# Chunk-end decays of a gated linear recurrence: one 32-partition transpose and four copies, against four transposes that write to their own partitions

## The chip, the cores and the metric

One core of one Trainium2 chip. The metric is the device time of one execution in microseconds (us), the median over several executions. The engines are TensorE (PE, with its weight loads shown apart as PEld), VectorE (DVE), ScalarE (ACT), GpSimd (POOL) and SyncE (SP); the last two issue most of the DMAs.

## The reference

```
batch, n_heads, seq, head_dim = (4, 8, 768, 48);  n_tokens, d_model, d_ff = (3072, 384, 2048)

state = zeros((B, H, D, D))
for t in range(S):
    state = alpha[:, :, t, :, None] * state + einsum('bhd,bhe->bhde', k[:, :, t], v[:, :, t])
    y[:, :, t] = einsum('bhd,bhde->bhe', q[:, :, t], state)

x = y.transpose(0, 2, 1, 3).reshape(B * S, H * D)
h = x @ w_in
g = 0.5 * h * (1.0 + tanh(sqrt(2 / pi) * (h + 0.044715 * h * h * h)))
return g @ w_out                                    # float32, 3072 x 384
```

A recurrence over 768 steps, in which each of the 48 features of a head decays by its own `alpha`, is followed by a two-layer feed-forward net.

## The kernel before

The sequence is cut into 6 chunks of 128 steps. A chunk of two batches is a unit; the 12 units have numbers m = 0 to 11 (chunk c = m // 2, batch pair i = m % 2), and a task's name holds its unit: `mask6.0` is the first mask of unit 6.

For one unit, ACT takes the logarithm of alpha (`ln`), PE sums it along the chunk (`cum`), ACT makes the running decay b = exp(cum) (`b`) and its inverse (`binv`), and DVE scales q by b (`qp`) and k by binv (`kp`). Both are turned so that features lie on partitions: on PE for units 0 to 4, by two DMA transposes issued from SP for units 5 to 11 (`turn`, line 546). PE makes the scores (`attn`, line 583; it also starts the outputs with the carried state, line 563), DVE masks them in four pieces (`mask`, line 590), PE finishes the outputs (`y`, lines 640 and 648), `x` copies them out of PSUM, and the turned x (`xT`) feeds layer 1 on PE (`l1`, line 683, 8 steps for each unit), ACT's `gelu` (line 689), and layer 2 on PE (`l2`, line 702, 8 steps for each unit), whose sums are copied out (`ot`, line 714) and stored from SP (`store`, line 727). `l16.2` is step 2 of layer 1 of unit 6.

The state is carried from chunk to chunk: PE makes k-transposed times v (`kv`, line 600), and DVE computes (kv + old state) * decay over the whole chunk (`st`, lines 622 and 625). That needs the last row of b with its features on partitions. For units 0 to 2 PE sums them in another way. For units 3 to 9 (`ROW_ENDS`) the task `rows` does it on DVE. b is a tile of 128 tokens by 768 values in float32; its last row is on partition 127. `row_ends` transposes the last 32 partitions in blocks of 32x32 into the tile `turned` (1024 elements on each of partitions 96 to 127), so that the last token becomes the last column of each block. Four copies (lines 467 and 468) then take these columns to partitions 0, 32, 64 and 96 of a small tile `rows`: even heads go to partitions 0 to 47, odd heads to 64 to 111. The task `end` (line 610) spreads the result over the two heads of a pair, and both `st` of the unit read that.

The order of the work on each engine is not written in loops: tasks with dependencies, costs and ranks go through a list scheduler when the kernel is built. The table `W` holds the cost it believes of each kind of task, `SHIFT` moves the rank of single tasks, `AFTER` adds dependencies that only fix an order, and `FIRST` writes out the order of roughly the first 40 us. Each engine then runs its own list in order. A task also waits for a buffer: `BUFS` gives the number for each tag. PSUM has four buffers of the tag `ff` (layer 1, layer 2 and half of the scores), two of `yk` (outputs, `kv`, turned x) and one double one of `ca`.

POOL issues the loads (line 337); before some of them it waits until a turned tile has landed (`gate`, line 351, steps such as 'hold k 8').

Of the kernel before, what the change touches and what calls it, by code (L numbers as in the profile page):

```python
# [7 lines left out]
F32 = mybir.dt.float32  # L8
# [8 lines left out]
    cum=530, cum_packed=1500, t8=450, t4=225, attn=340, kv=170, inter=165, intra=203, tx=168, l1_4=655, l1_2=340, l2=651,  # L17
    qk2=880, qk1=500, ev8=610, ev4=350, mask=610, st=1065, st0=545, end=110, attn2=600, vb=320, vb_act=480, ring=1300, ring_issue=670, out=2050, lead=600, receipt=1400, receipt_hw=1000, xc=475, xe=275, ot=540,
    ev8_act=920, ev4_act=520, xc_act=385, xe_act=400, ot_act=450,
    strip=1700, cast=1450, weight=2080, dma=2100, issue=1100, wissue=760, sp=420, store=2600, turn=1250, landed=2200, xbar_qk=1500, xbar_x=1400, turn_lead=50, stored=300, turn_receipt=200, rows=1600, ones=205, late_qk=1700, late_x=1700, late_x6=500, piece=330, late_k=1500, piece_issue=450, begin=620, cast_0=1300, share=1200, cast_1=1900, ln_packed=1040, cold=380, t64=640, fill=216, zero=1100,  # L20
)
COST = {
    ("ACT", "b"): (385, 135), ("ACT", "binv"): (385, 135), ("ACT", "ev"): (600, 40), ("ACT", "gelu"): (510, 110),
# [151 lines left out]
class _Kernel:  # L175
# [58 lines left out]
    PIECES = (0, 192, 320, 384)  # L234

    SHIFT = {
        'cum5.0': 100, 'ev4.1': 97, 'kp6.0': 1515, 'kp9.0': -3, 'kv3.0': -140, 'kv4.1': -540, 'mask3.0': 183, 'mask3.1': 300, 'mask6.3': 2077,
        'qp5.0': 1077, 'qp7.0': 57, 'qp8.0': 110, 'rows4.0': 450, 'rows7.0': -164, 'rows9.0': -280, 'tx3.1': -340, 'tx4.1': -727, 'x6.0': -7088,
        'x6.1': -7042,
    }  # L240

    AFTER = {
        'attn8.0': 'l17.2', 'kv6.1': 'l25.4',
    }

    ROW_ENDS = (3, 4, 5, 6, 7, 8, 9)

    URGENT = (2,)
    BUFS = dict(rows=3, turned=1, ca=1, yk=2, ff=4, la=3, qp=4, kp=4, b8=2, kn=2, qkT=4, atm=6, x=3, ot=4, bend=3, ends=8,
                a=5, q=5, k=5, vb=5)  # L250

    def __init__(self, ctx, tc, q, k, v, alpha, w_in, w_out, out):
        nc = self.nc = tc.nc
        self.tc, self.out = tc, out
        B, H, S, D = q.shape
        self.B, self.H, self.S, self.D = B, H, S, D
        C = self.C = 128
        self.NCH = S // C
        self.src = {"a": alpha, "q": q, "k": k, "v": v}
        self.w_in_dram, self.w_out_dram = w_in, w_out  # L260
        self.d_model, self.d_ff = w_in.shape
        self.NKT, self.NFT = self.d_model // C, self.d_ff // C

        self.const = ctx.enter_context(tc.tile_pool(name="const", bufs=1))
        self.sb = ctx.enter_context(tc.tile_pool(name="sb", bufs=1))
        self.ps = ctx.enter_context(tc.tile_pool(name="ps", bufs=1, space=bass.MemoryType.PSUM))

        const = self.const
        self.ut_h = const.tile([C, C], F16, name="ut_h")
        self.ut = const.tile([C, C], BF16, name="ut")  # L270
        self.gate = const.tile([C, 1], F32, name="gate")
        self.ut_blk = [const.tile([C, C], F16, name=f"ut_blk{i}") for i in range(2)]
        self.blk = const.tile([C, 4], F16, name="blk")
        self.ident = const.tile([C, C], BF16, name="ident")
        self.ones = const.tile([C, 1], F16, name="ones")
        self.zero = const.tile([C, 512], BF16, name="zero")
        self.half = const.tile([C, 2], F32, name="half")
        self.w_in = [const.tile([C, self.NKT, self.d_ff // 4], BF16, name=f"w_in{i}") for i in range(4)]
        self.w_out = const.tile([C, self.NFT, self.d_model], BF16, name="w_out")
        self.state = [[const.tile([C, H // 2, 2 * D], BF16, name=f"st{b}_{i}") for i in range(2)]  # L280
                      for b in range(B)]
        self.ring = {n: [const.tile([C, 2, H, 64], F16 if n == "la" else BF16, name=f"{n}{i}")
                         for i in range(self.BUFS[n])] for n in ("la", "qp", "kp")}
        self.used = {n: 0 for n in (*self.ring, "rows", "b")}
        self.bs = [const.tile([C, 2 * H * D + 16], F32, name=f"b{i}") for i in range(self.BUFS["b8"])]
        self.rows = [const.tile([C, 32], F32, name=f"rows{i}")[:, 0:H].rearrange("f (i p) -> f i p", i=2) for i in range(self.BUFS["rows"])]
        self.NX = 3
        self.xT = [const.tile([C, B, self.NKT, C], BF16, name=f"xT{c}") for c in range(self.NX)]
        self.NG = 2
        self.gT = [const.tile([C, self.NFT, B * C], BF16, name=f"gT{i}") for i in range(self.NG)]  # L290
        self.eng = {"ACT": nc.scalar, "DVE": nc.vector}

    def tile(self, tag, shape, dt, name=None):
        pool = self.ps if tag in ("ca", "yk", "ff") else self.sb
        return pool.tile(shape, dt, tag=tag, bufs=self.BUFS[tag], name=name or tag)

# [133 lines left out]
    def exp(self, u, n, lo, hi):  # L430
        D, H = self.D, self.H

        def emit(e):
# [7 lines left out]
            else:  # L441
                if n not in u:
# [4 lines left out]
                    else:  # L447
                        u[n] = self.sb.tile([self.C, 2, H, D], BF16, tag=n, bufs=self.BUFS["b8"], name=n)
                cum = u["cum"][lo][:, None, 0:H * D] if u["packed"] else u["cum"][:, lo:hi, 0:H * D]
# [4 lines left out]
    def row_ends(self, u):  # L454

        C, H, D = self.C, self.H, self.D
        nc = self.nc

        def emit(e):
            b, t = u["b_row"], self.tile("turned", [C, 2, H // 2, 2, 2, 32], F32, "b_turned")  # L460
            to = u["bend"] = self.rows[self.used["rows"] % len(self.rows)]
            self.used["rows"] += 1
            last = b[C - 32:C]
            nc.vector.transpose(t[C - 32:C].rearrange("t i p o b c -> t (i p o) b c"),  # L464
                                bass.AP(last.tensor, last.offset, [list(last.ap[0]), [D, 2 * H], [32, 2], [1, 32]]))
            for o in range(2):
                nc.vector.tensor_copy(to[64 * o:64 * o + 32], t[C - 32:C, :, :, o, 0, 31])
                nc.vector.tensor_copy(to[64 * o + 32:64 * o + D], t[C - 32:C - 32 + D - 32, :, :, o, 1, 31])
        return emit

    def scaled(self, u, n, lo, hi):
# [133 lines left out]
    def ends(self, u):  # L605
        C, H = self.C, self.H

        def emit(e):
            t = u["ends"] = self.tile("ends", [C, 2, H // 2, 2], F32)
            self.nc.vector.tensor_tensor(  # L610
                t.rearrange("f i p o -> f (i p) o"), u["bend"].rearrange("f i p -> f (i p)")[:, :, None].to_broadcast([C, H, 2]),
                self.half[:, None, :].to_broadcast([C, H, 2]), op=ALU.mult)
        return emit

# [115 lines left out]
    def tasks(self):  # L730
        s = self.s = Scheduler(self.BUFS, self.fill, 40000, self.FIRST, self.LANDED)
        B, NCH = self.B, self.NCH
# [283 lines left out]
    def run(self):  # L1016
        nc, C = self.nc, self.C
        self.tasks()
        nc.vector.memset(self.zero, 0.0)
        nc.vector.memset(self.ones, 1.0)  # L1020
        make_upper_triangular(nc, self.ut_h, val=1.0, diag=True)
        first = self.p[0, 0]["q"] = self.tile("q", [C, 2, self.H, self.D], F32)
        nc.vector.memset(first[:, 0, 0, 0:1], 0.0)
        make_identity(nc, self.ident)
        nc.vector.memset(self.half, 0.0)
        for o in range(2):
            nc.vector.memset(self.half[64 * o:64 * o + 64, o:o + 1], 1.0)
        nc.vector.tensor_reduce(self.blk, self.ident.rearrange("p (g j) -> p j g", j=4), axis=mybir.AxisListType.X, op=ALU.max)
        same = self.blk[:, None, :].to_broadcast([C, C // 4, 4])
        nc.vector.tensor_tensor(self.ut_blk[1].rearrange("p (g j) -> p g j", j=4), self.ut_h.rearrange("p (g j) -> p g j", j=4), same, op=ALU.mult)  # L1030
        nc.vector.tensor_tensor(self.ut_blk[0], self.ut_blk[1], self.ident, op=ALU.subtract)
        for i in range(max(self.BUFS[n] for n in self.ring)):
            for n in self.ring:
                if i < self.BUFS[n]:
                    nc.vector.memset(self.ring[n][i][:, :, :, self.D:64], 0.0)
        nc.vector.tensor_copy(self.ut, self.ut_h)
        for t in self.rows:
            nc.vector.memset(t, 0.0)
        for t in self.bs:
            nc.vector.memset(t[:, 2 * self.H * self.D:], 0.0)  # L1040
        order = self.s.order()
        for t in order:
            if t.load == LN_EXP:
                self.act_set(LN_EXP)
            t.emit(t.engine)
# [30 lines left out]
```

## Time and profile before

| what | value |
|---|---|
| median of three timed runs | 176.02 us (175.55, 176.02, 178.0) |
| profiled execution | 174.84 us, span 173.1 us, granted PE clock 1.000 |
| PE busy | 166.8 us, 96% of the span |
| ACT busy | 129.0 us, 75% |
| DVE busy | 105.2 us, 61%; nine tenths or more of nearly every slice from 47 to 74 us |
| POOL busy | 60.1 us, 35% |
| `rows`: 7 transposes | 8.7 us, 1241 ns each |
| `rows`: 28 copies | 6.0 us, 164 to 168 ns at the median, 880 ns at most |

The profile is one execution. The span runs from its first to its last instruction; the execution's own time is 1.74 us longer. In the timeline a group of matmuls is given with its modelled end, which reaches some 0.16 us past the start of the next group when PE runs without a gap: in such a row the next start, not the end, tells how fast PE goes. "Idle before" is counted from that modelled end.

### The profile page before, as it was taken

How to read it: one execution, taken by the hardware profiler on the slowest of the kernel's cores; microseconds unless marked ns; L12 is line 12 of the kernel's file. 1: busy time of each engine (PE TensorE's matmuls, PEld its weight loads, DVE VectorE, ACT ScalarE, POOL GpSimd, SP SyncE). 2: the span in 40 equal slices, each digit the busy share in tenths (PEclk: the TensorE clock that was granted, in tenths of full speed). 3: DMA queues.
4: the chain of work that ended last, by engine and by line, in shares of the span. 5: the costliest groups of instructions: out<-in, count | busy, mean ns of one | idle time of the engine just before them, and what ended most of it. 6: DMA issues, size and time to landing. Idle time of an engine off the chain costs nothing.

```text
span 173.1 us, 4474 instructions
## 1 busy us (share of the span) xinstructions
PE 166.8 (96%) x1847; PEld 130.2 (75%) x1847; DVE 105.2 (61%) x220; ACT 129.0 (75%) x212; POOL 60.1 (35%) x71
## 2 busy tenths in 40 slices
PE   7999999999999999999989999999999999999993
PEld 2666999666887795797777787787696796886973
DVE  6399920166889999895995697996950735100000
ACT  4578999756979888869679869868699892581831
POOL 2396446995645500810802503900800300000000
PEclk9999999999999999999999999999999999999999
DMA  4999999999999999799698996999899892401102
GB/s 135 308 252 214 203 241 236 239 228 203 228 301 198 255 238 110 138 204 163 166 246 135 165 218 141 169 252 204 185 174 167 97 177 48 119 18 45 49 0 91
DMA packets 54452, 30.11 MB, mean 174 GB/s; under 512 B 42528, under 2 KB 50848, under 8 KB 54432
## 3 DMA queue, kind: packets, MB, share of 16 engines
q0 software_dynamic: 26464, 17.70, 61.7%
q1 hardware_dynamic: 27424, 11.74, 33.9%
q10 hardware_dynamic: 544, 0.39, 0.9%
q8 instruction: 14, 0.23, 0.6%
q14 instruction: 6, 0.05, 0.1%
HBM read 25.17 MB, written 4.72 MB: 173 GB/s over the span
## 4 chain that ended last, share of the span: by engine, by line
PE 76%; DVE 10%; ACT 6%; DMA 3%; issue 2%; SPq 0%; DVEq 0%
PE hT L683 32%; PE acc L702 28%; PE at L583 3%; DMA a<-in_alpha_dram 2%; DVE b_turned L464 2%; DVE atm L590 2%; PE qkT_ps L488 2%; PE yps L648 2%; DVE stmp L622 1%; DVE st L625 1%; PE kv L600 1%; PE cum L416 1%; PE yps L563 1%; PE idle L318 1%; PE xT_ps L671 1%
## 5 line engine op out<-in xcount | busy, mean ns | idle before, releaser
L683 PE MATMUL hT<-xT,w_in 128*128 128x256 bf16 x576 | 68.2, 273 | 1.1 <-DVE atm L590 0.8
L702 PE MATMUL acc<-w_out,gT 128*128 128x384 bf16 (+3 forms) x416 | 68.8, 314 | 0.0
L689 ACT ACTIVATE gT<-hT 128x512 bf16<-128x512 f32 x96 | 55.4, 602 | 11.7 <-PE hT L683 8.0
L683 PEld LDWEIGHTS <-w_in 128*128 128x128 bf16 x576 | 61.4, 114 | 3.3 <-issue 1.4
L702 PEld LDWEIGHTS <-gT 128*128 128x128 bf16 x416 | 37.2, 98 | 19.6
L590 DVE TENSOR_TENSOR atm<-at,ut 128x512 bf16<-128x512 f32 x48 | 30.3, 683 | 4.8 <-PE at L583 4.6
L714 ACT COPY ot<-acc 128x384 f32<-128x384 f32 (+3 forms) x21 | 9.3, 446 | 17.2 <-PE acc L702 14.6
L351 POOL CAST gate<-qkT 128x1 f32<-128x1 bf16 x6 | 2.1, 353 | 51.4 <-DMA qkT<-kp 51.4
L478 DVE TENSOR_TENSOR kp<-k,binv 128x768 bf16<-128x768 f32 (+1 forms) x15 | 11.9, 793 | 11.0 <-ACT binv L450 10.6
L478 DVE TENSOR_TENSOR qp<-q,b 128x768 bf16<-128x768 f32 (+1 forms) x15 | 11.9, 792 | 8.4 <-ACT b L450 8.4
L337 POOL DMA_DIRECT2D k<-in_k_dram x11 | 12.2, 1108 | 6.0 <-DMA vb<-in_v_dram 3.3
L337 POOL DMA_DIRECT2D q<-in_q_dram x11 | 12.2, 1112 | 4.6 <-DMA k<-in_k_dram 1.2
L337 POOL DMA_DIRECT2D vb<-in_v_dram x11 | 12.3, 1116 | 3.8 <-PE kv L600 1.1
L337 POOL DMA_DIRECT2D a<-in_alpha_dram x11 | 12.3, 1115 | 3.5 <-DMA w_in<-in_moe_w_in_dram 1.3
L450 ACT ACTIVATE b<-cum 128x768 f32<-128x768 f32 (+1 forms) x15 | 10.3, 688 | 2.6 <-PE cum L418 1.5
L309 ACT ACT_TABLE_LOAD x9 | 11.5, 1283 | 0.9 <-PEq L1060 0.7
L689 ACT ACT_TABLE_LOAD x9 | 11.5, 1283 | 0.2
L622 DVE TENSOR_TENSOR stmp<-kv,st 128x384 f32<-128x384 f32 x16 | 8.9, 554 | 3.2 <-PE kv L600 3.0
L450 ACT ACTIVATE binv<-cum 128x768 bf16<-128x768 f32 (+1 forms) x15 | 10.3, 686 | 0.5 <-PE cum L388 0.5
L658 DVE CAST x<-yps 128x384 bf16<-128x384 f32 x9 | 4.9, 556 | 8.2 <-PE yps L648 8.2
L464 DVE STREAM_TRANSPOSE b_turned<-b 32x1024 f32<-32x1024 f32 x7 | 8.7, 1241 | 1.7 <-ACT b L450 1.6
L625 DVE TENSOR_TENSOR st<-stmp,ends 128x384 bf16<-128x384 f32 x16 | 8.9, 558 | 0.6
(86 smaller groups left out, 152.8 us busy)
## 6 DMA issues: line engine op xcount, KB each, us to landing
out_dram<-ot SPq DMA_DIRECT2D x19, 192.0 KB, 3.7
a<-in_alpha_dram POOLq DMA_DIRECT2D x9, 384.0 KB, 8.9
q<-in_q_dram POOLq DMA_DIRECT2D x9, 384.0 KB, 8.6
k<-in_k_dram POOLq DMA_DIRECT2D x9, 384.0 KB, 7.0
vb<-in_v_dram POOLq DMA_DIRECT2D x9, 192.0 KB, 9.6
w_in<-in_moe_w_in_dram POOLq DMA_DIRECT2D x4, 384.0 KB, 9.3
w_out<-in_moe_w_out_dram POOLq DMA_DIRECT2D x4, 384.0 KB, 11.1
out_dram<-ot SPq DMA_DIRECT2D x9, 96.0 KB, 4.6
```

Of the source, the lines that this page charges most:

```text
L309: nc.scalar.add_instruction(mybir.InstLoadActFuncSet(name=nc.get_next_instruction_name(), act_func_set_id=i, engine=mybir.EngineType.Activ ...
L337: dma(u[t][:, lo:hi].rearrange("t b h d -> t (b h) d"), src.rearrange("b h s d -> s (b h) d")[c * C:(c + 1) * C])
L450: self.nc.scalar.activation(u[n].rearrange("t i h d -> t i (h d)")[:, lo:hi], cum, AF.Exp, scale=1.0 if n == "b" else -1.0)
L464: nc.vector.transpose(t[C - 32:C].rearrange("t i p o b c -> t (i p o) b c"), bass.AP(last.tensor, last.offset, [list(last.ap[0]), [D, 2 * ...
L478: self.nc.vector.tensor_tensor(out, rows, b, op=ALU.mult)
L590: self.nc.vector.tensor_tensor(u["atm", i][:, o], u["at", i][o], self.ut[:, None, :].to_broadcast([self.C, self.H // 2, self.C]), op=ALU.mult)
L622: nc.vector.tensor_tensor(s, acc, old, op=ALU.add)
L625: nc.vector.tensor_tensor(new.rearrange("f p (o d) -> f (p o) d", o=2), acc.rearrange("f p (o d) -> f (p o) d", o=2), ends, op=ALU.mult)
L683: self.nc.tensor.matmul(h[:, s], w_in[:, j, nt % 4 + s], self.xT[c % self.NX][:, lo:hi, j], start=j == 0, stop=j == self.NKT - 1, skip_gro ...
L689: return lambda e: self.nc.scalar.activation(self.gT[c % self.NG][:, nt:nt + 2, lo * self.C:hi * self.C], f.pop(("h", c, lo, nt)), AF.Gelu ...
L702: self.nc.tensor.matmul(f["acc", c, b][:, lo:hi], self.gT[c % self.NG][:, nt, b * self.C:(b + 1) * self.C], self.w_out[:, nt, lo:hi], star ...
L714: self.copy(e)(f["ot", c, b][:, sl], f["acc", c, b] if half is None else f["acc", c, b, half][:, sl])
```

## The change

The transpose and the four copies of `row_ends` become four transposes. Each takes the 32 values of one half (features 0 to 31 or 32 to 63; the second half runs into the next head's values, as before) of all 8 even or all 8 odd heads, reads them in steps of two heads, 256 elements on each of 32 partitions, and writes straight to the partitions of `rows` where these features belong. `rows` grows to 128 x 8 x 32; the decays are its last column, [:, :, 31], which `end` now reads in steps of 32 elements. The tile `turned` and the clearing of `rows` at the start go.

The cost of `rows` in the scheduler's table goes from 1600 to 1400, and `SHIFT` and `AFTER` are new, so the order of tasks changes on PE, DVE, ACT and SP from about 52 us on. POOL's order stays, and so does all that `FIRST` writes out.

```diff
-        'cum5.0': 100, 'ev4.1': 97, 'kp6.0': 1515, 'kp9.0': -3, 'kv3.0': -140, 'kv4.1': -540, 'mask3.0': 183, 'mask3.1': 300, 'mask6.3': 2077,
-        'qp5.0': 1077, 'qp7.0': 57, 'qp8.0': 110, 'rows4.0': 450, 'rows7.0': -164, 'rows9.0': -280, 'tx3.1': -340, 'tx4.1': -727, 'x6.0': -7088,
-        'x6.1': -7042,
+        'b10.0': 10, 'binv8.0': -10, 'ev4.1': -154, 'kp6.0': 1801, 'kp7.0': -13, 'kp9.0': -347, 'ln5.0': -1426, 'mask10.0': -50, 'mask3.1': 340,
+        'mask8.0': 200, 'mask8.1': 36, 'qp4.0': -217, 'qp5.0': 10, 'qp8.0': 10, 'st4.0': 870, 't4.0': -633,
...
-        'attn8.0': 'l17.2', 'kv6.1': 'l25.4',
+        'b4.0': 'binv4.0', 'kv8.1': 'l27.2',
...
-        self.rows = [const.tile([C, 32], F32, name=f"rows{i}")[:, 0:H].rearrange("f (i p) -> f i p", i=2) for i in range(self.BUFS["rows"])]
+        self.rows = [const.tile([C, H, 32], F32, name=f"rows{i}") for i in range(self.BUFS["rows"])]
...
-            b, t = u["b_row"], self.tile("turned", [C, 2, H // 2, 2, 2, 32], F32, "b_turned")
-            to = u["bend"] = self.rows[self.used["rows"] % len(self.rows)]
+            t = self.rows[self.used["rows"] % len(self.rows)]
             self.used["rows"] += 1
-            last = b[C - 32:C]
-            nc.vector.transpose(t[C - 32:C].rearrange("t i p o b c -> t (i p o) b c"),
-                                bass.AP(last.tensor, last.offset, [list(last.ap[0]), [D, 2 * H], [32, 2], [1, 32]]))
+            last = u["b_row"][C - 32:C]
             for o in range(2):
-                nc.vector.tensor_copy(to[64 * o:64 * o + 32], t[C - 32:C, :, :, o, 0, 31])
-                nc.vector.tensor_copy(to[64 * o + 32:64 * o + D], t[C - 32:C - 32 + D - 32, :, :, o, 1, 31])
+                for half in range(2):
+                    f = 64 * o + 32 * half
+                    nc.vector.transpose(t[f:f + 32], bass.AP(last.tensor, last.offset + o * D + 32 * half,
+                                                             [list(last.ap[0]), [2 * D, H], [1, 32]]))
+            u["bend"] = t[:, :, 31]
...
+            last = u["bend"] if u["m"] in self.ROW_ENDS else u["bend"].rearrange("f i p -> f (i p)")
             self.nc.vector.tensor_tensor(
-                t.rearrange("f i p o -> f (i p) o"), u["bend"].rearrange("f i p -> f (i p)")[:, :, None].to_broadcast([C, H, 2]),
+                t.rearrange("f i p o -> f (i p) o"), last[:, :, None].to_broadcast([C, H, 2]),
...
-        for t in self.rows:
-            nc.vector.memset(t, 0.0)
```

The pieces of the new order that the prediction uses, each engine's list read from left to right:

```
DVE before: rows3 st2.1 mask3.2 mask3.3 end3 mask3.0 mask3.1 st3.1 xe3.1 qp4 kp4 xe3.0 st3.0 rows5 ev4.0 kp5 ev4.1 end5 rows4 mask4.0-4.3 end4
DVE after:  rows3 st2.1 mask3.0 mask3.2 mask3.3 end3 mask3.1 x3.1 x3.0 kp4 qp4 xe3.1 rows4 ev4.1 ev4.0 end4 kp5 st3.0 st3.1 rows5 mask4.0-4.3
DVE before: st5.0 st5.1 rows7 mask6.0-6.2 kp7 end7 qp7 mask6.3 x6.0 st6.0 rows8 st6.1 ot5.1 kp8 mask7.0-7.3 end8 qp8
DVE after:  st5.0 st5.1 kp7 qp7 mask6.0-6.3 rows7 x6.1 end7 st6.0 st6.1 kp8 rows8 mask7.0-7.3 qp8 x7.0 end8
DVE before: st8.0 st8.1 rows9 ot6.1 kp9 qp9 end9 mask8.0-8.3
DVE after:  st8.0 mask8.2 mask8.3 mask8.1 mask8.0 ot6.1 x8.0 kp9 qp9 rows9 end9
PE before:  l16.0 l16.1 attn7 l16.2-16.4 l16.5 l16.6 y7 l16.7 l26.0 kv7.0 kv7.1 l26.1 l26.2 kv8.0 l26.3 cum9 kv8.1 l26.4-26.7 l17.0-17.3 attn8
PE after:   attn7 l16.0-16.4 y7 l16.5 l16.6 kv7.0 kv7.1 l16.7 l26.0 kv8.0 l26.1-26.3 attn8
SP before:  turn8 (k), turn8 (q), turn7 (x)          SP after: turn8 (k), a store of unit 5, turn8 (q), turn7 (x)
```

## The prediction

> **What bounds the kernel now.** I read the page first, then PE's timeline for places where it waits, then DVE's and POOL's for the reason, then SP's.
>
> ```profile
> span 173.1 us, 4474 instructions
> ...
> PE 166.8 (96%) x1847; PEld 130.2 (75%) x1847; DVE 105.2 (61%) x220; ACT 129.0 (75%) x212; POOL 60.1 (35%) x71
> ...
> L464 DVE STREAM_TRANSPOSE b_turned<-b 32x1024 f32<-32x1024 f32 x7 | 8.7, 1241 | 1.7 <-ACT b L450 1.6
> ```
>
> PE sets the end. A cut in DVE time is worth only what PE loses to DVE. PE's timeline shows where that is:
>
> ```profile
> 67.58 0.86 PE L648 MATMUL yps<-vb,atm 128*128 128x48 bf16 x16
> ...
> 69.61 0.33 PE L671 MATMUL xT_ps<-ident,x 128*128 128x128 bf16 x3 [0.18 <-DVE x L658]
> ...
> 87.79 4.09 PE L683 MATMUL hT<-xT,w_in 128*128 128x256 bf16 x36 [0.79 <-DVE atm L590]
> ...
> 100.18 0.60 PE L583 MATMUL at<-qkT 64*128 64x128 bf16 x15 [0.17 <-DVE ot L714]
> ...
> 113.72 0.81 PE L683 MATMUL hT<-xT,w_in 128*128 128x256 bf16 x6 [0.30 <-DVE ot L714]
> ```
>
> The printed idle time starts at a modelled end, 0.16 us after the point where the next group could have started, so each wait costs 0.16 more: 0.34, 0.95, 0.33 and 0.46. The first row, y4, lasts 0.86 where the later groups of this kind last 0.56: 0.30 of waiting inside it. With 0.20 at 94.89 (where `cum8` waits for ACT) PE loses 0.30 + 0.34 + 0.95 + 0.33 + 0.46 + 0.20 = 2.58 us after 50 us. After 114 us it loses nothing to DVE. That is the ceiling of any gain here, 1.5% of the time.
>
> The two largest losses stand behind `rows`:
>
> ```profile
> 84.32 1.24 DVE L464 STREAM_TRANSPOSE b_turned<-b 32x1024 f32<-32x1024 f32 x1
> 85.60 0.16 DVE L467 COPY rows<-b_turned 32x8 f32<-32x8 f32 x1
> 85.77 0.16 DVE L468 COPY rows<-b_turned 16x8 f32<-16x8 f32 x1
> 85.95 0.88 DVE L467 COPY rows<-b_turned 32x8 f32<-32x8 f32 x1
> 86.84 0.17 DVE L468 COPY rows<-b_turned 16x8 f32<-16x8 f32 x1
> ```
>
> POOL's timeline at the same time:
>
> ```profile
> 85.67 1.16 POOL L337 DMA_DIRECT2D a<-in_alpha_dram  x1
> ```
>
> The third copy ends at 86.83, exactly with this POOL row. A copy at 111.92 (0.80 us) ends likewise at 112.72 with the POOL row of 111.57. The transpose of 110.47 lies wholly under POOL rows and takes its usual 1.24.
>
> **What one `rows` costs.** Before: five of the seven run 2.01 us from first start to the next instruction's start (59.16 to 61.17), the two with a blocked copy 2.72 and 2.64.
>
> After: four transposes of 32x256; no row shows one. DVE's time grows by 1.04 ns for each element (kp: 553 ns for 384 elements, 953 for 768), so the transpose of 1024 is 1065 + 176 fixed, and one of 256 is 266 + 176 = 442 ns. Do neighbours overlap? The copies, with no wait between the last three, start 0.17 to 0.18 apart while each lasts 0.16 to 0.17: no overlap. Memsets at the start do overlap:
>
> ```profile
> 2.62 0.17 DVE L1035 MEMSET la<- 128x128 uint32 x1
> 2.76 0.17 DVE L1035 MEMSET qp<- 128x128 uint32 x1
> ```
>
> The copies write to different groups of 32 partitions in turn; the memsets don't. The four transposes do as the copies, so I take no overlap and a gap of 0.015: 4 x 0.457 = 1.83 us, 0.18 less than 2.01. With the overlap of the masks (0.08 a piece) it would be 4 x 0.36 = 1.45. Outer bounds: 4 x 0.31 = 1.24, if a quarter of the elements takes a quarter of the time, and 4 x 1.24 = 4.96 if size didn't matter, which the kp rows speak against; the latter, behind which three `rows` stand before y4, would lose PE some 15 us.
>
> The Trainium skill (VectorE: DVE Perf Modes, section "Two Vector instructions with no wait between them") says that an instruction whose output starts in another quadrant than the last one's waits until all earlier ones are done. That speaks against the change: the splitting into four pays the fixed part four times. By it the sum is 1.83, without it 1.45.
>
> The same skill (SBUF — State Buffer, section "Who interferes with whom") lists copies among the operations that lock a port shared with GpSimd, one blocking the other; it doesn't list the transpose there. By it the 0.7 us accidents go with the copies; else they may return.
>
> **What goes and what stays, with the new order.** Times are those of the trace, shifted by each edit.
> - `rows7` is no longer ahead of `mask6.0`. Instead kp7 and qp7 are (0.87 each): 84.30 + 1.75 = 86.05, mask done 86.74; layer 1 needs its buffer at 86.84. Loss 0.95 becomes 0.
> - `ot6.1` no longer stands behind `rows9` (it precedes it): 0.46 becomes 0. `ot5.1` goes from behind `rows8` to ACT, and `cum8` comes one step later, when its input is there: 0.33 and 0.20 become 0.
> - y3.1's mask3.3 comes third: 51.93 - 0.18 + 2 x 0.60 + 0.68 + 0.06 (release) = 53.69 against 53.63: 0.06.
> - Ahead of unit 4's masks, DVE gets two casts from ACT (x3, 0.46 each), gives up one `xe` (0.27), and saves 0.18 on each of rows3, 4 and 5: +0.11. y4's loss goes from 0.30 to 0.41; the 0.34 behind it stays. No gain in the stretch where DVE is fullest.
> - `rows7` now stands between mask6.3 (88.46) and x6.1: x6.1 is done 88.46 + 1.83 + 0.55 = 90.84; kv6.1, which needs its buffer, could go at 90.67. New loss, with release, 0.23.
> - `rows8` now stands between kp8 and mask7.0. cum8 is one layer-2 step (0.65) and one kv (0.17) later, and so are ACT's exponentials: kp8 ends 98.2, rows8 100.03, mask7.0 100.71. attn7 has moved ahead of l16.0 and starts at 98.18, so l16.2 wants mask7.0's buffer at 100.24: new loss 0.46.
> - The cleared `rows` tiles (three memsets, 0.1 us) lie in DVE's free time from 4.3 to 6.5; `end` reads as many elements as before.
>
> Sum: 0.06 + 0.41 + 0.34 + 0.23 + 0.46 = 1.50 lost in place of 2.58: 1.1 us gained, 174.84 to 173.7 on the profiled execution (span 172.0, and the 1.74 around it as before). That one is 1.2 us below the median of the timed runs, 176.02, and below all three; I carry the difference over: 174.9.
>
> **Rivals.**
> 1. The transposes overlap (1.45). Three rows of 0.38 less take y4's loss and most of the 0.34 behind it away, kv6.1's too, and l16.2's falls to 0.08: some 0.3 left, 2.3 gained, 173.7 at the median. For it: nothing depends on a neighbour; against: the copies.
> 2. No cheaper: with 2.01 for one `rows` the losses are 0.24 + 0.95 + 0.34 + 0.41 + 0.64 = 2.58: no change, 176.0. For it: each instruction pays the fixed part.
> 3. Slower, by one mechanism: attn8 waits for its turned q. It moves ahead by ten PE steps. Before, SP issued that turn at 104.36, it landed 2.7 us later, and attn8 went at 114.68: 7.6 us to spare. After, from the end of mask7.0, DVE has three masks and qp8 ahead of the turn, 2.8 us; PE has six layer-1 steps, y7, four layer-2 steps and three kv, 3.93 + 0.40 + 2.60 + 0.51 = 7.44. PE waits if landing takes over 4.6 us, and the kernel gets slower than before from 5.7.
>
> ```profile
> 104.36 1.23 SPq L546 DMA_TRANSPOSE qkT<-qp  x1
> ```
>
> The fourteen turns land in 2.7 to 7.7 us, the slow ones with loads on the queues. At 7.7 the price is 3.1 - 1.1 = 2.0: 178.0. A store now goes between the two turns of unit 8, which speaks for it; against it, the loads of that time (k9, issued at 96.6, 6.6 us) have nearly landed, and the next ones are held until unit 8's k has. I expect about 4. The turns of unit 11 meet the same rule: attn11 moves ahead by one step of 0.65, of 1.1 to spare; both late would make 179.5 or more.
>
> **How the numbers follow.** Chances: forecast 0.45, rival 1 0.14, rival 2 0.12, rival 3 0.29. The time is the forecast's, 174.9. The range goes down to rival 1 with 1.2 us for the runs' excess over the profiled one, 172.5, and up over 178.0 towards both turns late, 178.6. The bound of 2%, about what a measurement of this kernel can tell from no change, is 3.5 us. Faster by that needs rival 1 and a steadier course of the runs: 0.15. Slower by it needs rival 3 at both places, or more at one: 0.23. The rest, 0.62, is within.
>
> **What would show it.** A 32x256 transpose of 0.44 us, with starts 0.46 apart (0.36: rival 1); none longer under POOL's rows. The 14.7 us that DVE is busy in `rows` (8.7 + 6.0) become 28 x 0.442 = 12.4. PE's waits at 87 and 113 us are gone, y4's stays, a small one before l16.2 is new. A PE wait at attn8 released by the DMA of qkT is rival 3. The forecast is wrong if PE's new waits sum to over 2.6 us, or if a wait appears that no piece above names.

## The result, and the profile after

The changed kernel takes 174.26 us at the median of 18 runs, the kernel before 175.16 beside it; the ratio is 0.994 (95% interval 0.9915 to 0.9966). That is 1.0 us less (0.6 to 1.5), inside the bound of 2%. Forecast were 1.1 us less, and 174.9. The ratios, here and below, leave out the executions that took over 1.5% longer than the fastest of their kernel, most of them at a granted clock of 0.99 or less; the medians include them.

The page of the profiled execution (174.67 us, 0.17 less than the one before):

```profile
span 172.9 us, 4460 instructions
...
PE 164.6 (95%) x1845; PEld 129.8 (75%) x1847; DVE 102.9 (59%) x209; ACT 129.0 (75%) x213; POOL 59.4 (34%) x71
...
L465 DVE STREAM_TRANSPOSE rows<-b 32x256 f32<-32x256 f32 x28 | 12.3, 438 | 0.5
```

28 transposes at 438 ns, 12.3 us in all: the forecast had 442 and 12.4. DVE's timeline shows how closely they follow each other:

```profile
49.10 1.79 DVE L465 STREAM_TRANSPOSE rows<-b 32x256 f32<-32x256 f32 x4
50.92 0.56 DVE L622 TENSOR_TENSOR stmp<-kv,st 128x384 f32<-128x384 f32 x1
```

Four in 1.79, and 1.82 to the next instruction's start: no overlap, as taken. The same holds for the other six `rows`. Nine of the 28 transposes overlap a DMA row of POOL, and none is longer for it: the shortest of all takes 435 ns and the longest 442.

PE's timeline at the places of before:

```profile
67.83 0.82 PE L648 MATMUL yps<-vb,atm 128*128 128x48 bf16 x16
...
69.81 0.49 PE L671 MATMUL xT_ps<-ident,x 128*128 128x128 bf16 x6 [0.18 <-DVE x L658]
...
85.69 3.47 PE L683 MATMUL hT<-xT,w_in 128*128 128x256 bf16 x30
...
91.08 0.50 PE L599 MATMUL kv<-vb,kp 128*128 128x96 bf16 x8 [0.20 <-DVE x L658]
...
99.66 3.44 PE L683 MATMUL hT<-xT,w_in 128*128 128x256 bf16 x30 [1.15 <-DMA xT<-x]
```

y4 and x4 lose nearly as before (0.82 against 0.56, and 0.18 + 0.16). The wait at 87 us is gone: 30 matmuls run through. The ones at 100 and 113 us are gone too. kv6 has its new wait of 0.20 + 0.16. And one wait stands here that no step of the prediction named: layer 1 of unit 6 waits 1.15 + 0.16 us for its turned x. With 0.04 at y3.1 (lines not shown) the losses in this profile sum to 2.31 us: 0.27 less than before, where 1.1 were forecast.

### The profile page after: what moved, and what is told of

Read it like the earlier page. It is cut to its first block, busy times and chain, and to the rows that moved or that the text cites. A ratio compares the mean times of both kernels' runs of the same rounds, so it can differ in the third digit from the quotient of the medians.

```text
span 172.9 us, 4460 instructions
## 1 busy us (share of the span) xinstructions
PE 164.6 (95%) x1845; PEld 129.8 (75%) x1847; DVE 102.9 (59%) x209; ACT 129.0 (75%) x213; POOL 59.4 (34%) x71
## 4 chain that ended last, share of the span: by engine, by line
PE 73%; DVE 14%; DMA 8%; issue 2%; ACT 1%; SPq 0%
PE hT L683 31%; PE acc L702 28%; DMA xT<-x 5%; DVE atm L589 3%; DVE rows L465 3%; PE at L582 3%; DMA a<-in_alpha_dram 3%; DVE qp L477 2%; PE kv L599 2%; PE yps L648 1%; PE qkT_ps L487 1%; DVE kp L477 1%; PE cum L415 1%; DVE stmp L622 1%; DVE st L625 1%
## 5 line engine op out<-in xcount | busy, mean ns | idle before, releaser
L689 ACT ACTIVATE gT<-hT 128x512 bf16<-128x512 f32 x96 | 54.7, 603 | 8.4 <-PE hT L683 5.1
L350 POOL CAST gate<-qkT 128x1 f32<-128x1 bf16 x6 | 1.6, 261 | 49.1 <-DMA qkT<-kp 49.1
L336 POOL DMA_DIRECT2D a<-in_alpha_dram x11 | 12.3, 1115 | 4.3 <-DMA w_in<-in_moe_w_in_dram 1.7
L465 DVE STREAM_TRANSPOSE rows<-b 32x256 f32<-32x256 f32 x28 | 12.3, 438 | 0.5
## 6 DMA issues: line engine op xcount, KB each, us to landing
w_out<-in_moe_w_out_dram POOLq DMA_DIRECT2D x4, 384.0 KB, 11.1
```

The lines of the kernel that those rows point to most:

```text
L336: dma(u[t][:, lo:hi].rearrange("t b h d -> t (b h) d"), src.rearrange("b h s d -> s (b h) d")[c * C:(c + 1) * C])
L465: nc.vector.transpose(t[f:f + 32], bass.AP(last.tensor, last.offset + o * D + 32 * half, [list(last.ap[0]), [2 * D, H], [1, 32]]))
L689: return lambda e: self.nc.scalar.activation(self.gT[c % self.NG][:, nt:nt + 2, lo * self.C:hi * self.C], f.pop(("h", c, lo, nt)), AF.Gelu ...
```

## The experiments

Two theories. A: `rows` became cheaper and lost its accidents with POOL, which is the gain, and the new order gives part of it back, because it was laid out for a `rows` of 1.40 us. B: the new order brings the gain. All ratios are to the kernel before on the same chip.

**The transposes in the old order.** The changed kernel with the old `SHIFT` and `AFTER` and, in the cost table:

```diff
-... rows=1400, ...
+... rows=1600, ...
```

> The four transposes in the old order (old ranks, old cost in the table), nothing else. Theory A, the cheaper rows bring the gain and the new order gives part of it back: with 1.83 us for one rows and no blocked copy the old places of loss shrink: y4 and x4 0.64 to 0 (three rows of 0.18 less ahead of them), 87 us 0.95 to 0, 100 us 0.33 to 0.15, 113 us 0.46 to 0, cum8 0.20 stays: 0.35 in place of 2.58, so 2.2 us below before (ratio 0.987) and about 1 us below the changed kernel. Rival B, the new order brings the gain: this kernel stays within 0.4 us of before. If a transposes' load jam at 98 us belongs to the new order, PE waits for no DMA here.

Measured: 173.2 us, 0.9884 (0.9847 to 0.9921). Run again with the last two orders below, on another chip:

> The four transposes in the old order once more, beside the other two on the same chip: ratio 0.988 to before, again with PE's losses behind y4, at 87 and at 113 us gone.

Measured: 173.23 us, 0.9891 (0.9838 to 0.9943). PE's timeline of the first:

```profile
67.28 0.57 PE L649 MATMUL yps<-vb,atm 128*128 128x48 bf16 x16
...
68.01 0.81 PE L703 MATMUL acc<-w_out,gT 128*128 128x384 bf16 x4
68.92 0.33 PE L672 MATMUL xT_ps<-ident,x 128*128 128x128 bf16 x3
...
84.83 5.47 PE L684 MATMUL hT<-xT,w_in 128*128 128x256 bf16 x48
...
98.22 0.80 PE L583 MATMUL at<-qkT 64*128 64x128 bf16 x16
```

y4 takes 0.57, and layer 1 of unit 5 runs through in one piece of 48 matmuls where PE stood for 0.95 us. Three units' `rows` of 0.18 less each were enough for y4. Not all of the 0.64 there went: x4 starts 0.91 us after a group that takes 0.65 without a gap, a loss of 0.26 that is too short to be printed as a wait. With 0.20 at attn7 (0.80 where its like take 0.60) and 0.20 at cum8, 0.66 us are left in both profiles, not the 0.35 expected. From 2.58 that makes 1.92 us of gain, and the ratios say 2.0 and 1.9. A wait of 0.81 for the turned x of unit 9, at 135.7 us, stands in this profile and not in the second one, which has one of 0.16, at 142.0 us, for the turned k of a later unit: waits for turned tiles are not the new order's alone. So the transposes alone gain at least as much as the whole change. That they gain more is what the waits say; the ratios of the two overlap (see the changed kernel once more, below).

**The copies in the new order.** The kernel before with the changed kernel's `SHIFT`, `AFTER` and `rows=1400`.

> The new order (new ranks, new cost in the table) with the old transpose and four copies. Theory A: with 2.01 us for one rows the losses of the new order sum to 2.6 us, as many as before: ratio 1.000, and up to 0.7 us more for each copy that a POOL DMA row blocks ahead of something PE waits for. Rival B, the new order brings the gain: 1 us below before, like the changed kernel (ratio 0.994). Copies of over 0.7 us, if any, end when a DMA row of POOL ends.

Measured: 1.0003 (0.997 to 1.0036). No gain: B falls. PE's timeline holds the losses that a `rows` of 2.01 us makes in this order, of which two are:

```profile
91.85 0.50 PE L599 MATMUL kv<-vb,kp 128*128 128x96 bf16 x8 [0.39 <-DVE x L657]
...
101.21 2.13 PE L682 MATMUL hT<-xT,w_in 128*128 128x256 bf16 x18 [0.49 <-DVE atm L589]
```

0.55 at kv6 (rival 2 of the prediction had 0.41) and 0.65 at l16.2 (0.64). With 0.22 at y3.1, 0.57 at y4, 0.34 at x4 and 0.38 at 75 us, where layer 1 waits for an `ot` on DVE, they sum to 2.71, against the 2.58 of the old order. One copy lasted 0.35 us here, to 72.77, the end of a POOL row (71.61, 1.16 long); none of 0.7 occurred.

**The changed kernel once more.**

> The changed kernel as it is, beside the others on the same chip: 0.994 of before. In its profile the wait of layer 1 for xT of unit 6 is there again (over 0.5 us) if it belongs to the order, and absent if the first profile was an accident.

Measured: 0.9908 (0.9872 to 0.9944), which overlaps with 0.994 (0.9915 to 0.9966), and with the old order's 0.9884 (0.9847 to 0.9921) beside it. Its PE timeline:

```profile
90.83 0.50 PE L599 MATMUL kv<-vb,kp 128*128 128x96 bf16 x8 [0.20 <-DVE x L658]
...
98.20 1.50 PE L683 MATMUL hT<-xT,w_in 128*128 128x256 bf16 x12
100.00 2.12 PE L683 MATMUL hT<-xT,w_in 128*128 128x256 bf16 x18 [0.30 <-DVE atm L589]
```

Layer 1 of unit 6 starts at 98.20 without the wait for xT, and now l16.2 waits for mask7.0, 0.30 + 0.16 = 0.46, exactly the term of the prediction, which the longer wait of the first profile had covered.

**What delays the turned x.** In the changed kernel SP issues the turns of unit 7 at 85.4 and 87.4 us (before: 89.9 and 92.3), into the loads that POOL issues from 83.5 to 87. They land 6.9 and 9.2 us after their issue (before: 3.7 and 2.8), and the turn of x6, issued at 91.08 behind them, after 8.5 (before: 2.8). SP's timeline, of the kernel before and then of the changed one:

```profile
89.86 2.37 SPq L546 DMA_TRANSPOSE qkT<-kp  x1
92.32 1.26 SPq L546 DMA_TRANSPOSE qkT<-qp  x1
93.68 1.24 SPq L552 DMA_TRANSPOSE xT<-x  x1
```

```profile
85.41 1.26 SPq L545 DMA_TRANSPOSE qkT<-kp  x1
...
87.40 3.50 SPq L545 DMA_TRANSPOSE qkT<-qp  x1
91.08 3.90 SPq L551 DMA_TRANSPOSE xT<-x  x1
```

The transposes in the old order lie between: with the same loads, their turns of unit 7 leave at 88.3 and 89.6 us and land after 5.5 and 5.1. Two runs looked for what delays them. First, SP issued x6 ahead of the q of unit 7:

```diff
         order = self.s.order()
+        late = next(t for t in order if t.name == "turn7.0")
+        order.remove(late)
+        order.insert(1 + next(i for i, t in enumerate(order) if t.name == "turn6.2"), late)
```

> The changed kernel with one step moved: SP issues the turn of q of unit 7 after the turn of x of unit 6, not before. Theory: in the changed kernel's profile PE waits 1.15 us at 98 us for xT of unit 6, because the turns of unit 7 were issued some 5 us earlier than before, into the loads of 83 to 87 us, and the turn of x stands behind them on SP. Then that wait goes here; l16.2's wait for mask7.0, hidden so far, shows up with about 0.5 us; the sum is 0.5 to 0.8 us below the changed kernel where that wait is typical, 0 where the profiled execution was unlucky. Rival: the loads themselves delay the turn of x, whatever stands ahead of it: the wait stays within 0.3 us of what it was.

Measured: 0.9948 (0.9911 to 0.9985): no gain over the changed kernel. In its profile (granted clock 0.989) the wait for xT is gone, and attn7 waits 2.68 us for the q of unit 7 instead, which was issued 4.4 us later than in the changed kernel and landed 8.0 us after that. In this one profile the order on SP only chose which of the two is late. Second, the loads that POOL issues from 93 us on were held until x6 had landed:

```diff
         order = self.s.order()
+        next(t for t in order if t.name == "gate.4").emit = self.hold("x", 6)
```

> The changed kernel with one thing altered: POOL's gate ahead of the loads v8, q9, k9 waits for the turned x of unit 6, not for the turned k of unit 7. Theory: these loads, issued from 93 us on, share the queues with the turns of unit 7 and of x6 and delay them; then the turn of x6 lands some 3 us after its issue (5.3 to 8.5 in the changed kernel), PE never waits for it, and the time is 0.2 to 0.6 us below the changed kernel. Rival: the loads issued before, from 83 to 87 us, delay the turns: the landing stays above 5 us and the time is the same or, with loads later, longer.

It has no ratio, so what it does to the time isn't shown; the profiled execution took 174.62 us. The turn of x6 still landed only after 5.0 us, k and q of unit 7 after 5.6 and 7.9, though the held loads went out only at 96.1 us, when all three had landed: the later loads are not what delays them, and the theory falls. That the earlier ones (83 to 87 us) do is what remains; it was not shown by taking them away. Nor is it known why x6 took 8.5 us in the first profile of the changed kernel and 5.3 in the second. The run showed something else, in PE's timeline and SP's:

```profile
108.46 0.37 PE L562 MATMUL yps<-st,qkT 64*128 64x48 bf16 x16 [1.34 <-DMA qkT<-qp]
```

```profile
102.13 1.28 SPq L545 DMA_TRANSPOSE qkT<-qp  x1
```

The held loads now went out from 96.1 to 99.6 us (93.0 to 96.5 in the changed kernel), nearer to the turn of q of unit 8, which landed at 108.4, 6.3 us after its issue, and attn8 waited 1.34 + 0.16 = 1.50 us. This is the prediction's third rival at its place: a wait from 4.6 us of landing on, 6.3 - 4.6 = 1.7 by its sum. In the changed kernel's two profiles the same turn landed after 3.6 and 3.3 us, and attn8 did not wait.

**Why the four don't overlap.** All four transposes write to partitions 96 to 127, of four tiles, so three quarters of the decays are left at zero.

```diff
+            to = [t, *(self.rows[(self.used["rows"] + i) % 3] for i in range(2)), self.spare]
...
-                    nc.vector.transpose(t[f:f + 32], ...
+                    nc.vector.transpose(to[2 * o + half][C - 32:C], ...
```

> The changed kernel and its order, with all four transposes writing to partitions 96 to 127 (of four different tiles), so that three quarters of the decays are left at zero. Theory A (writing to another group of 32 partitions than the instruction before makes each transpose wait for the end of the last): here the second, third and fourth start 0.35 to 0.37 us after the one before, one rows takes 1.45 to 1.5 in place of 1.82, and since the new order was laid out for 1.40, its own losses (y4 and x4, kv6, l16.2: 1.3 us) shrink to 0.4 or less: 0.8 to 1.2 us below the changed kernel, 0.985 of before. Rival: the gap comes from the transposes themselves: starts stay 0.45 apart and the time stays that of the changed kernel.

Measured: 0.9856 (0.9792 to 0.9921), 0.9 to 1.5 us below the changed kernel's two values, with intervals that overlap. DVE's timeline shows the overlap itself:

```profile
48.54 1.10 DVE L467 STREAM_TRANSPOSE rows<-b 32x256 f32<-32x256 f32 x3
49.57 0.40 DVE L467 STREAM_TRANSPOSE spare<-b 32x256 f32<-32x256 f32 x1
50.00 0.56 DVE L624 TENSOR_TENSOR stmp<-kv,st 128x384 f32<-128x384 f32 x1
```

Starts are (49.57 - 48.54) / 3 = 0.343 us apart, not 0.45, and one `rows` takes 1.46 us, not 1.82, in all seven: the sum that the prediction gave for overlap was 1.45. The source was the same in both, partitions 96 to 127; the place of the output changed, its partitions and its tile. Another tile alone doesn't bring the overlap: behind the fourth transpose DVE goes on in one more tile, on partitions that begin at 0, and starts 0.43 us after a transpose of 0.40, in all seven `rows`. This is the rule of the Trainium skill that the prediction set against the change (VectorE: DVE Perf Modes, "Two Vector instructions with no wait between them"), with its price here: 0.11 us for each transpose that follows another. In this profile y3.1, y4, x4 and kv6 don't wait for DVE: at 1.46 us for one `rows`, near the 1.40 of the table, these losses of the new order are gone. l16.2 can't be judged, because PE comes late to it: it waits 5.27 us for the turned q of unit 7 and 1.74 for the turned x of unit 6 (granted clock of this execution: 0.972).

**The lock.** The kernel before, with four more copies and four 32x32 transposes behind each of the seven `rows`.

```diff
+            for i in range(4):
+                nc.vector.tensor_copy(self.spare[32 * (i % 2):32 * (i % 2) + 32, 0:8]..., t[C - 32:C, :, :, 0, 0, 31])
+                nc.vector.transpose(self.spare[64 + 32 * (i % 2):96 + 32 * (i % 2)], t[C - 32:C, 0, 0, 0, 0, :])
```

> The kernel before, with four more copies of the same form and four 32x32 transposes, in turn, behind each of the seven rows (their results are not used). A look at the lock alone, the time doesn't count. Theory: a copy takes 0.16 us, or it lasts longer and then ends within 0.03 us of the end of a DMA row of POOL (one or more of the 56 copies); no transpose lasts longer, under a POOL row or not. Rival: long ones occur anywhere, among transposes too.

DVE's timeline and POOL's:

```profile
123.46 0.82 DVE L469 COPY rows<-b_turned 16x8 f32<-16x8 f32 x1
...
124.66 0.79 DVE L471 COPY spare<-b_turned 32x8 f32<-32x8 f32 x1
125.48 0.21 DVE L472 STREAM_TRANSPOSE spare<-b_turned 32x32 f32<-32x32 f32 x1
```

```profile
123.16 1.16 POOL L338 DMA_DIRECT2D k<-in_k_dram  x1 [0.40 <-issue]
124.31 1.15 POOL L338 DMA_DIRECT2D a<-in_alpha_dram  x1
```

Three of 56 copies are long (the third, at 51.57, lasts 0.78), and each ends 0.01 to 0.04 us before a POOL row does. In the three profiles with copies 13 overlap a POOL row, and six of them are long; why the other seven aren't is open. The 28 small transposes take 205 to 209 ns, the seven large ones 1241 to 1242. Only two of the small ones overlap a POOL row, too few to tell. But of the large ones 13 of 21 do, in three profiles, all at 1241 or 1242 ns, and of the transposes of 32x256 88 of 224, in the eight profiles that write them to four places, all from 435 to 443. The list of the Trainium skill (SBUF — State Buffer, "Who interferes with whom") agrees with the copies; that the transpose stays out of it is what these rows add.

**Orders for the true cost.** 1830 in the cost table and ranks searched anew, twice.

> The four transposes with a third order: the scheduler's table holds 1830 for rows, near the 1.82 us that the traces show, and the ranks were searched anew for it, so that no PE step is placed ahead of what it needs from DVE. If DVE's lateness is all that PE loses, some 0.1 us of the 2.58 us of losses remain: 2.4 us below before (ratio 0.986), 0.2 to 0.4 us below the transposes in the old order. Rival: the turns' landings, which the ranks trust to be steady, give it back: ratio 0.988 or more.

> As the run before, with ranks from another search: the same expectation, ratio 0.986 (rival 0.988 or more). Two searches, because each order has its own places where a turn is late.

Measured: 0.9838 (0.9761 to 0.9915) and 0.9935 (0.9899 to 0.9971), against 0.9891 (0.9838 to 0.9943) for the old order beside them. In the first one's profile PE's timeline prints no wait after 50 us. But its interval holds the old order's value, and the second missed the 0.986 that was expected and is no better than the changed kernel: the tie between these orders isn't broken. The second one's profile (granted clock 0.990) has waits of 1.18 and 3.32 us for a turned x; whether they are why its ratio is higher, the rival that was named, isn't shown. The version to keep is the four transposes in the old order, which beat the kernel before in both of its measurements.

## Why the prediction was right

- *PE sets the end, and 2.58 us of losses to DVE and ACT are the ceiling.* The transposes in the old order gain 2.0 and 1.9 us, and their waits fall by 1.92. The two lowest ratios, 0.9838 and 0.9856, are 2.8 and 2.5 us, and the interval of the first holds the ceiling's 0.985.
- *One `rows` costs 1.83 us.* Measured 1.82. The place of the output decides, as the copies against the memsets had told; with that out of the way it is 1.46.
- *New losses of 1.50 us.* In the first profile of the changed kernel they are 2.31, with a wait that has no term in the sum. In the second they are, in the prediction's order, y3.1 0.04 (0.06 forecast), y4 0.26 (0.41), x4 0.34 (0.34), kv6 0.36 (0.23), l16.2 0.46 (0.46): 1.46. y4's term was too large by 0.15 and kv6's too small by 0.13.
- *The 1.1 us gained.* Measured 1.0 (0.6 to 1.5). That it came out so near is in part luck: the two profiles of the changed kernel lose 0.27 and 1.12 us less than the one before. Of the two parts that the prediction added up, the cheaper `rows` brings 2.0 us in the old order, and the new order gains nothing with copies. So the losses at 87 and 113 us, which the prediction took away by moving work from behind `rows`, go without the moves as well. How much of the 2.0 the new order gives back is less sure: 0.4 to 1.0 us by the ratios (0.9908 and 0.994 against 0.9884 and 0.9891), whose intervals overlap on the one chip that had both; the 0.36 at kv6 and 0.46 at l16.2 are its own, and the old order's profile has neither.
- *The carry-over of 1.2 us from the profiled execution to the median* was too much: over more runs the median before was 175.16, 0.3 above the profiled one. The forecast of 174.9 is 0.6 too high for that.
- *Rival 1* (overlap) fell by the starts 0.45 apart, *rival 2* (no cheaper) by the 1.82 and the old order's 0.9884. *Rival 3* didn't occur at attn8 in the changed kernel's profiles (3.6 and 3.3 us of landing, about 4 expected), and did where the loads were moved against it.
- *What the prediction missed*: the same kind of delay one unit earlier. It priced `rows7`'s move behind kp7 and qp7 by DVE alone. The turns that follow these two left 4.5 and 4.9 us earlier as well, into the loads, and the turn of x6 queued behind them. That took 1.31 us in the first profile and nothing in the second. A wait that no piece names was one of the prediction's own signs of being wrong, and the first profile shows it; the forecast of the time held all the same.
- *The outer bound of 4.96 us.* The 15 us that PE would lose are not worked out: three `rows` of 2.95 us more are 8.9. Nothing else rests on them.

## What to carry to other kernels

Before an instruction is split into several, look in the trace whether neighbours that write to different groups of 32 partitions overlap: here they didn't, and the split saved 0.19 us of one `rows` where 0.55 were to be had with overlap. An order made for a cost that is not reached places work ahead of what it needs: measure the new part in the old order first. Whether ranking anew with the measured cost then gains more was not settled here. When a step moves forward, every transfer that it triggers moves too: follow these to the queue, and ask what stands behind them there.

## What the runs showed of the hardware beyond that

A transpose's time on DVE goes with the elements of a partition: 207 ns for 32x32, 438 for 32x256, 1241 for 32x1024, so 1.03 to 1.05 ns an element above a fixed part. It is also shorter behind another that writes to the same partitions: 0.40 us in place of 0.44 for the same 256 elements. A transpose by DMA of the same size (the turned q or k of a unit) landed anywhere from 2.7 to 11.1 us after its issue in these profiles, and SP was held up to 4.9 us in issuing one; in the profile with the granted clock of 0.972 one took 15.4 us, and SP was held for 5.8 in issuing a turned x.
